# Key-value products beside the rows of the second layer, copied by ScalarE

## The chip, the cores and the metric

The kernel runs on one core of a Trainium2 chip. The metric is the device time of one execution in microseconds (us).

## The reference

Eight batches of eight heads, 576 positions, head size 64, go through an attention without softmax and a root-mean-square norm. The 8 x 576 = 4608 rows of 512 values that come out of it go through two dense layers with a gate.

```python
kv  = einsum('bhsd,bhse->bhde', k, v)            # 64x64 a head
out = einsum('bhsd,bhde->bhse', q, kv)
x   = out / sqrt(mean(out * out, -1) + 1e-6) * g_norm   # heads side by side: 4608 x 512
h   = x @ w_in                                   # 512 x 2048
y   = (h * sigmoid(1.702 * h)) @ w_out           # 2048 x 512
```

## The kernel before

**Stages.** Stage t = 0 to 8 (`for t in range(NT)`) computes both layers of 512 rows. Stages 0 to 7 take the first 512 positions of batch t; stage 8 takes the 64 remaining positions (the remainder) of all eight batches. Beside its layers, stage t does the attention of batch b = t + 1, so that its rows are ready when the next stage begins. Most of a stage is one long order of TensorE (PE) instructions, written out by hand: `at1(n, f)` puts work behind step n of the first layer, `at2(n, f)` behind step n of the second. Every engine takes its instructions in program order, and a wait on one holds back all that stands behind it on the same engine.

**First layer** (`hid_seven`, from stage 1 on). Seven products in place of eight, as in Strassen's scheme, for each of four groups of columns: 28 products of four matmuls of 256 columns. The list of a `Plan` names them: "21" is product 1 of group 2. Product 1 leaves a snapshot of its PSUM bank (copied by VectorE or ScalarE, letter by letter in `snap`) to which product 2 adds; product 5 leaves one for the sum that 6 completes; products 2, 3, 4 and 7 are followed by a gate on ScalarE (L539). `xsums` tells behind which steps VectorE forms the four sums of x (xS, L491); product 5 reads the first and product 6 the second. The word "kv" in the list is the place of the key-value products. `SECOND` is the plan of stage 1, `LATER` of stages 2 to 6, `LAST_TWO` of stages 7 and 8.

**Second layer** (`Seven.run`). Seven products of two halves of eight matmuls, 112 steps. `place` adds up and writes the output block; the last, behind step 111, is a ScalarE copy (L659). `ready` and `later` place VectorE's sums of the gated values (gS, L611).

**Attention of a batch from 2 on.** GpSimd's queue loads k, v and q as f16 (`load_kv`, `load_q`), into one buffer for k and one for v, and two for q, taken in turn. `transpose_q` turns q by a DMA of SP's queue. The 40 key-value products (L238: per head pair four blocks of 128 positions and the remainder, 128x64 weights, two heads side by side in the 64-column halves) go to one PSUM bank `kvp`. `keep_kv` copies it in four pieces into `kvd[b % 2]`. `rows` multiplies the turned q with it: 32 matmuls with 64x128 weights (L313) into four banks. ScalarE squares them (L323), VectorE adds up (`add_up`), ScalarE takes the reciprocal roots (`roots`, L338), VectorE scales (`turn`, L341), and two DMA transposes on SP's queue (L347) give `xT`, which the next stage reads. The remainder has its own path: `out` (L287), a square, `ss` (a matmul with ones, L358), a root on ScalarE (L360), `apply` on VectorE (L374), at steps 46, 74 and 80. Roots and gates need different tables of ScalarE, so that two `preload_act_table_set` stand in each second layer, the one for the gates at step 82.

**PSUM.** `ps_a` ("a") and `ps_h` ("h") have three banks each and `ps_o` ("o") two. `kvp`, one bank of the rows, the bank y of the second layer, `out`, `ss` and four banks of the first layer share `ps_a`.

**Where the moved work stands before.** For batch b, "kv" is the third entry of `LATER` (behind 21 and 01) and the 23rd of `SECOND`; the four copies follow on VectorE. Right behind, from step 15 (23) of the same first layer, stand `load_kv(t + 2)` and `load_q(t + 2)`; GpSimd holds them back until the products have read the buffers. The attention object of batch t + 2 is made and its q is turned at step 100 of the second layer.

Of the kernel before, what the change touches and what calls it, by code (L numbers as in the profile page):

```python
# [7 lines left out]
F16 = mybir.dt.float16  # L8
F32 = mybir.dt.float32
# [3 lines left out]
P = 128  # L13
# [3 lines left out]
def kernel(  # L17
# [52 lines left out]
    ident = const.tile([P, P], F16)  # L70
    ones2 = const.tile([P, P], F16)
    eps_t = const.tile([P, 1], F32)
    g_col = const.tile([P, 1], F32)
    w_in_sb = const.tile([P, KO, DFF], F16)
    w_out_sb = const.tile([P, FO, DM], F16)
# [32 lines left out]
    RW = J * D  # L108
    RS = H * RW

    def load_kv(b, h0=0, h1=H, rest=True):

        for n in "kv":
            nc.gpsimd.dma_start(  # L114
                out=kv_rows[n][:, h0 * RW : h1 * RW].rearrange("p (h x) -> p h x", x=RW),
                in_=srcs[n][b, h0:h1, 0:SM, :].rearrange("h (p j) d -> p h (j d)", j=J),
            )
        for n in "kv" if rest else "":
            nc.gpsimd.dma_start(
                out=kv_rows[n][0:R, RS : RS + H * D].rearrange("p (h d) -> p h d", d=D),  # L120
                in_=srcs[n][b, :, SM:S, :].rearrange("h p d -> p h d"),
            )

    def clear_rest():
        for n in "kv":
# [85 lines left out]
    class Attention:  # L211
# [3 lines left out]
        def __init__(self, b):  # L215
            self.b, self.kb = b, kvb[b] if b < EARLY else kvd[b % 2]
            self.qT, self.o = {}, {}
            x = xpool.tile([P, KO * SM], F16, name="xT", tag="xT")
            if b < EARLY:
                self.x = xT[b] = x.rearrange("p (c n) -> p c n", c=KO)  # L220
            else:
                self.x = x.rearrange("p (m r) -> p m r", r=P)
                xT[b] = x.rearrange("p (j c r) -> p c j r", j=J, c=KO)
                self.x16 = attn.tile([P, J, DM], F16, name="x16", tag="x16", bufs=1)

        def kv(self, c):
            if c % self.KEEP == 0:
# [18 lines left out]
        def early_kv_product(self, t, c):  # L246
            for j in range(NJ):
                for hl in range(2):
# [6 lines left out]
                        stop=(j == NJ - 1),  # L255
                    )

        def kv_all(self, engine):
            self.engine = engine
            for c in range(NPAIR):  # L260
                self.kv(c)

        def keep_kv(self, c0, c1):

# [24 lines left out]
        def out(self, c):  # L289
            pool, tag = (ps_a, "att") if c < NPAIR else self.rest_pool  # L290
            t = pool.tile([P, SM], F32, name="outT", tag=tag)
            if c < NPAIR:
                n = SM
                self.product(t, c)
            else:
                n = NPAIR * R
                for i in range(NPAIR):
                    self.rest_product(t[:, i * R : (i + 1) * R], i)
            t = t[:, 0:n]
            sq = attn.tile([P, SM], F16, name="sq", tag="sq", bufs=3)  # L300
            nc.scalar.activation(sq[:, 0:n], t, AFT.Square)
            self.o[c] = (t, sq, n)

        def rows(self, i):

            t = [
                pool.tile([P, DM], F32, name="outR", tag=tag)
                for pool, tag in ROW_BANKS[i]
            ]
            for h in range(H):  # L310
                for half in range(2):
                    r = slice(half * D, (half + 1) * D)
                    nc.tensor.matmul(  # L313
                        t[half][:, h * D : (h + 1) * D],
                        self.qTd[r, h * (J // 2) + i, :],
                        self.kb[r, h // 2, half, 1 - h % 2, :],
                        start=(h == 0),
                        stop=True,
                        skip_group_check=True,
                    )  # L320
            for half in range(2):
                sq = attn.tile([P, SM], F16, name="sq", tag="sq", bufs=3)
                nc.scalar.activation(sq, t[half], AFT.Square)  # L323
                self.o[2 * i + half] = (t[half], sq)

# [12 lines left out]
            nc.scalar.activation(s4, s4, AFT.Abs_reciprocal_sqrt, bias=eps_t, scale=1.0 / D)  # L338

        def turn(self, j):  # L340
            nc.vector.tensor_mul(  # L341
                self.x16[:, j, :].rearrange("p (h d) -> p h d", d=D),
                self.o[j][0].rearrange("p (h d) -> p h d", d=D),
                self.sum4[:, j, :].unsqueeze(2).to_broadcast([P, H, D]),
            )
            if j % 2:
                nc.sync.dma_start_transpose(  # L347
                    out=self.x[:, (j - 1) * KO : (j + 1) * KO, :],
                    in_=self.x16[:, j - 1 : j + 1, :].rearrange("p j n -> p (j n)"),
                )  # L350
# [541 lines left out]
    for fo in COLS[4:GROUP]:  # L892
# [28 lines left out]
        {'rows': (19, 19), 'add_up': (22, 26, 27, 31), 'table': 26, 'roots': (27, 33), 'turn': (40, 50, 51, 52)},  # L921
    )
    LATER = Plan(
# [4 lines left out]
        {1: 'DAAA', 5: 'AAAD'},  # L928
        "D",
        "aooa",  # L930
        "aahh",
        {15: '34'},
        (0, 1, 6, 11),
        {'rows': (15, 15), 'add_up': (17, 20, 24, 28), 'table': 24, 'roots': (28, 39), 'turn': (35, 38, 46, 48)},
    )
    LAST_TWO = Plan(
# [21 lines left out]
    for t in range(NT):  # L958
# [12 lines left out]
        if t == 0:  # L971
            for l in range(2):
                at1(6, nc.vector.memset, kvd[l], 0.0)
            at1(7, of(0, "out", NPAIR))
            at1(7, scale_w_in, 0, 4)
            at1(7, w_in_sums, 0, 2)
            at1(8, start, 1)
            at1(12, scale_w_in, 4, 6)
            at1(12, w_in_sums, 2, 3)
            at1(13, load_q, 2)  # L980
            at2(4, setattr, a0, "ss_pool", Attention.ss_pool)
            at2(4, of(0, "ss", NPAIR, True))
            at2(4, of(0, "apply", NPAIR))
            at2(18, weight_sum, 0, 0, HF)
            at2(18, scale_w_in, 6, 8)
            at2(18, w_in_sums, 3, 4)
            for c in range(NPAIR):
                at1(12, of(1, "pack_q", c))
                at2(9 + 3 * c, of(1, "q", c))
                at2((36, 36, 49, 49)[c], of(1, "kv", c))  # L990
                at2((41, 43, 54, 55)[c], of(1, "out", c))
                at2((45, 50, 58, 60)[c], of(1, "ss", c))
                at2((48, 52, 58, 62)[c], of(1, "apply", c))
            for n in range(1, 4):
                at2(19, weight_sum, n, 0, 4)
                at2(38, weight_sum, n, 4, 6)
            at2(39, load_kv, 2, 0, H // 2, False)
            at2(51, clear_rest)
            at2(51, load_kv, 2, H // 2, H)

            def first_sum():
                made[1] = Sums(1, xT[1])
                made[1].form(0)

            at2(55, first_sum)
        elif b < B:
            todo = plan(t)
            at1(todo.steps.index("kv"), of(b, "kv_all", todo.keep))
            if t == 1:
                at1(5, start, b)  # L1010
                at1(5, of(b, "transpose_q"))
                at1(4, nc.scalar.preload_act_table_set, "gelu_apprx_sigmoid_and_others")
                for n, i in ((1, 8), (2, 11), (3, 16)):
                    at1(i, weight_sum, n, 6, HF)
            if t + 2 < B:
                late = max(15, todo.steps.index("kv") + 1)
                at1(late, load_kv, t + 2)
                at1(late, load_q, t + 2)
                at2(100, start, t + 2)
                at2(100, of(t + 2, "transpose_q"))  # L1020
            at = todo.attn
            at2(at["table"], nc.scalar.preload_act_table_set, "abs_reciprocal_sqrt_and_small")
            for h in range(2):
                at2(at["roots"][h], of(b, "roots", h))
            for j in range(J):
                if j < J // 2:
                    at2(at["rows"][j], of(b, "rows", j))
                for name in ("add_up", "turn"):
                    at2(at[name][j], of(b, name, j))
            at2(46, of(b, "out", NPAIR))  # L1030
            at2(74, of(b, "ss", NPAIR))
            at2(80, of(b, "apply", NPAIR))
            at2(82, nc.scalar.preload_act_table_set, "gelu_apprx_sigmoid_and_others")
        elif t < B:
            for name in ("ss_pool", "rest_pool"):
                at2(16, setattr, live[1], name, (ps_a, "att"))
            at2(16, of(1, "out", NPAIR))
            at2(34, nc.scalar.preload_act_table_set, "abs_reciprocal_sqrt_and_small")
            at2(44, of(1, "ss", NPAIR))
            at2(50, of(1, "apply", NPAIR))  # L1040
            at2(52, nc.scalar.preload_act_table_set, "gelu_apprx_sigmoid_and_others")
# [31 lines left out]
```

## Time and profile before

| what | us |
|---|---|
| median of 3 runs | 259.71 |
| lowest, highest | 259.07, 260.14 |
| the profiled execution | 259.19 |
| its span in the trace | 257.4 |

The profile shows one execution. PE is the matmul, PEld the weight load that overlaps it, DVE is VectorE, ACT ScalarE, POOL GpSimd, SP SyncE; a "q" behind the name is the engine's queue of DMA issues. The granted clock of TensorE was 1.00 throughout. In the chain of waits a line is: start, length, engine and place, number of instructions. In a timeline it is the same with the operation, its operands and, in square brackets, the engine's idle time before it and who ended it; matmuls overlap, so that a timeline's group ends with its last matmul and the next group may start before. The chain counts a matmul from when its predecessor hands over, some 0.16 us after its start in the timeline. The lines on DMA issues end with the median time from issue to landing.

### The profile page before, as it was taken

To read this page: it belongs to the slowest core of one execution; us is meant where nothing else is said; L and a number is where in the kernel's file an instruction comes from. 1 tells how busy PE (TensorE), PEld (TensorE's weight loads), DVE (VectorE), ACT (ScalarE), POOL (GpSimd) and SP (SyncE) were. 2 spreads that over 40 slices of the span, in tenths; PEclk is the share of its full clock that TensorE was granted. 3 is DMA by queue.
4 is the path that set the end of the run, shared out by engine and by line. 5 is a ranking of instruction groups with operands and counts; after the bars stand their busy time and mean duration, and the time that the engine had idled before them with its cause. 6 is when DMAs were issued, how large, how long until landed. Compare 5 with 4: busy or idle time off the path is not lost.

```text
span 257.4 us, 6356 instructions
## 1 busy us (share of the span) xinstructions
PE 250.0 (97%) x2596; PEld 203.3 (79%) x2596; DVE 195.1 (76%) x351; ACT 175.0 (68%) x315; POOL 55.9 (22%) x85
## 2 busy tenths in 40 slices
PE   7889999999999999999999999999999999999994
PEld 2434454788888888888888888888888888888883
DVE  1565686899968896889689968996899687557842
ACT  3477834988749974997499748984799469836820
POOL 8963245107025002600160007000000000000013
PEclk9999999999999999999999999999999999999999
DMA  7999999999989947994799579957600430012005
GB/s 169 198 201 205 205 203 197 231 201 136 165 183 172 216 65 172 144 229 62 176 141 226 60 177 140 230 58 175 165 4 0 84 163 3 0 60 107 3 17 147
DMA packets 68671, 35.33 MB, mean 137 GB/s; under 512 B 37954, under 2 KB 66242, under 8 KB 68386
## 3 DMA queue, kind: packets, MB, share of 16 engines
q0 software_dynamic: 37616, 18.31, 54.9%
q1 hardware_dynamic: 30624, 16.29, 27.1%
q8 instruction: 20, 0.33, 0.5%
q10 hardware_dynamic: 402, 0.33, 0.4%
q14 instruction: 9, 0.07, 0.1%
HBM read 36.70 MB, written 9.44 MB: 179 GB/s over the span
## 4 chain that ended last, share of the span: by engine, by line
PE 92%; DMA 5%; POOL 1%; issue 0%; DVE 0%
PE o L679 38%; PE h L559 38%; PE o L794 5%; PE hT L452 5%; DMA w_in_sb<-in_moe_w_in_dram 3%; DMA qraw<-in_q_dram 2%; PE kvp L238 2%; PE outR L313 1%; PE ss L358 1%; POOL w_in_sb L171 0%; PE q L433 0%; PE kvp L250 0%; PE outT L283 0%; PE outT L287 0%; POOL vbuf L90 0%
## 5 line engine op out<-in xcount | busy, mean ns | idle before, releaser
L539 ACT ACTIVATE gT<-h 128x512 f16<-128x512 f32 x96 | 52.5, 602 | 5.4 <-PE h L559 5.3
L559 PEld LDWEIGHTS <-ws 128*128 128x128 f16 x512 | 50.1, 98 | 5.8
L679 PEld LDWEIGHTS <-gS 128*128 128x128 f16 x512 | 49.4, 98 | 6.2 <-DVE gS L611 0.3
L559 PE MATMUL h<-xS,ws 128*128 128x256 f16 x384 | 52.2, 273 | 0.0
L679 PE MATMUL o<-tw,gS 128*128 128x256 f16 x384 | 46.5, 273 | 0.0
L679 PEld LDWEIGHTS <-gT 128*128 128x128 f16 x384 | 37.6, 98 | 4.3
L559 PEld LDWEIGHTS <-w_in_sb 128*128 128x128 f16 x384 | 37.1, 98 | 4.7
L559 PE MATMUL h<-xT,w_in_sb 128*128 128x256 f16 x224 | 31.9, 273 | 0.0
L679 PE MATMUL o<-w_out_sb,gT 128*128 128x256 f16 x256 | 31.4, 273 | 0.0
L573 DVE TENSOR_TENSOR h<-h,s 128x512 f32<-128x512 f32 x32 | 22.2, 697 | 6.7 <-PE h L559 5.5
L114 POOL DMA_DIRECT2D kraw<-in_k_dram x7 | 6.0, 855 | 90.4 <-PE kvp L238 86.2
L575 DVE TENSOR_TENSOR s<-h,s 128x512 f32<-128x512 f32 x32 | 22.1, 691 | 4.1 <-PE h L559 3.3
L656 DVE TENSOR_TENSOR osb<-o,qf 128x512 f32<-128x512 f32 (+1 forms) x25 | 16.7, 668 | 11.2 <-PE o L679 8.3
L713 POOL DMA_DIRECT2D out_dram<-osb x6 | 3.2, 541 | 90.9 <-DVE osb L656 90.9
L611 DVE TENSOR_TENSOR gS<-gT 128x512 f16<-128x512 f16 (+2 forms) x32 | 21.2, 684 | 0.6 <-ACT gT L539 0.6
L539 ACT ACTIVATE gT<-s 128x512 f16<-128x512 f32 x32 | 19.8, 628 | 2.6 <-DVE s L575 2.5
L559 PE MATMUL h<-xS,w_in_sb 128*128 128x256 f16 x128 | 18.9, 273 | 0.0
L360 ACT ACTIVATE rs<-ss,eps_t 128x512 f32<-128x512 f32 (+1 forms) x16 | 9.2, 582 | 13.6 <-PE ss L358 13.5
L966 ACT ACT_TABLE_LOAD x14 | 18.0, 1283 | 0.3
L648 ACT COPY qf<-o 128x512 f32<-128x512 f32 (+1 forms) x26 | 14.2, 547 | 4.5 <-PE o L679 4.4
L329 DVE TENSOR_REDUCE sum<-sq 128x8 f32<-128x512 f16 x24 | 15.3, 679 | 2.5 <-ACT sq L323 2.5
L509 ACT COPY h<-h 128x512 f32<-128x512 f32 x27 | 15.6, 585 | 2.1 <-PE h L559 2.0
(100 smaller groups left out, 361.0 us busy)
## 6 DMA issues: line engine op xcount, KB each, us to landing
out_dram<-osb SPq DMA_DIRECT2D x8, 512.0 KB, 3.8
kraw<-in_k_dram POOLq DMA_DIRECT2D x5, 512.0 KB, 9.2
vbuf<-in_v_dram POOLq DMA_DIRECT2D x5, 512.0 KB, 12.2
out_dram<-osb SPq DMA_DIRECT2D x2, 1024.0 KB, 4.9
qraw<-in_q_dram POOLq DMA_DIRECT2D x3, 512.0 KB, 13.5
qbuf<-in_q_dram POOLq DMA_DIRECT2D x3, 512.0 KB, 13.5
out_dram<-osb SPq DMA_DIRECT2D x6, 192.0 KB, 5.6
w_in_sb<-in_moe_w_in_dram POOLq DMA_DIRECT2D x2, 512.0 KB, 10.8
```

Of the source, the lines that this page charges most:

```text
L329: nc.vector.tensor_reduce(out=self.sum4[:, j, :], in_=self.o[j][1].rearrange("p (x d) -> p x d", d=D), op=ALU.add, axis=mybir.AxisListType.X,)
L452: nc.tensor.matmul(self.h[fo], w_in_sb[:, ko, fo * P : (fo + 1) * P], self.x[:, ko], start=(ko == 0), stop=(ko == KO - 1),)
L509: (nc.vector.tensor_copy if engine == "D" else nc.scalar.copy)(to, src)
L539: nc.scalar.activation(self.gT[:, to, n * TH : (n + 1) * TH], src, AFT.Gelu_apprx_sigmoid)
L559: nc.tensor.matmul(bank[name][:, a], w, x, start=(p in (1, 5) and a == 0 and k == 0), stop=(k == KH - 1), skip_group_check=True,)
L573: nc.vector.tensor_add(bank["z"], bank["x"], self.s5)
L575: nc.vector.tensor_add(self.s5, bank["x"], self.s5)
L611: op(s[:, n, lo], a, b)
L648: nc.scalar.copy(self.kept[as_][:, m], ps)
L656: nc.vector.tensor_add(o, ps, self.kept[with_][:, m])
L679: nc.tensor.matmul(o, a, w, start=(p in (1, 2, 5) and i == 0 and (mo == 0 or split)), stop=(i == HF - 1), skip_group_check=True,)
L966: u2.setdefault(i, []).append(lambda: f(*args))
```

## The change

The products of batches 4 to 7 move from the first layer of stages 3 to 6 to step 15 of the second layer of stages 2 to 5, directly ahead of the rows of batches 3 to 6. Their bank is copied at step 52, by ScalarE. Batch 3 has its products and copies (by ScalarE) at step 88 of stage 1's second layer; batch 2 stays where it is. In `LATER`, "kv" is gone and 25 stands ahead of 22; the second roots come at step 29 (before: 39), and one of VectorE's gS sums at 29 (before: 22). In stages 2 to 5 the remainder's four steps move from 46, 74, 80, 82 to 80, 90, 96, 97. The loads change their place: k of batch t + 3 behind the products at step 15, then at step 101 a one-element GpSimd copy that reads the last block of the turned rows (`after_turn`, so that the queue waits for that transpose), and behind it v, the two remainders and q. The squares get a fourth buffer, and `x16` is allocated with its first use.

```diff
-    def load_kv(b, h0=0, h1=H, rest=True):
+    def load_kv(b, h0=0, h1=H, rest=True, main="kv"):
-        for n in "kv":
+        for n in main:
...
+    def after_turn(b):
+        nc.gpsimd.tensor_copy(out=mark, in_=xT[b].rearrange("p c j r -> p j c r")[0:1, J - 1, KO - 1, 0:1])
...
+        def kv_products(self):
+            self.kvp = ps_a.tile([P, NPAIR, D], F32, name="kvp", tag="att")
+            for c in range(NPAIR):
+                self.kv_product(self.kvp[:, c, :], c)
+        def kv_copies(self, engine):
+            self.engine = engine
+            self.keep_kv(0, NPAIR)
         def kv_all(self, engine):
-            self.engine = engine
-            for c in range(NPAIR):
-                self.kv(c)
+            self.kv_products()
+            self.kv_copies(engine)
...
     LATER = Plan(
-        "21 01 kv 22 05 25 06 11 02 15 26 03 16 12"
+        "21 01 25 22 05 06 11 02 15 26 03 16 12"
         " 07 31 27 13 17 35 36 04 23 24 32 33 14 37",
-        {23: ((0, 4, 0), (0, 4, 1)), 26: ((4, 6, 0),)},
-        {0: ((0, 8, 2),), 16: ((4, 8, 1),), 22: ((4, 8, 3),), 58: ((0, 4, 3),)},
+        {22: ((0, 4, 0), (0, 4, 1)), 25: ((4, 6, 0),)},
+        {0: ((0, 8, 2),), 16: ((4, 8, 1),), 29: ((4, 8, 3),), 58: ((0, 4, 3),)},
...
-        (0, 1, 6, 11),
+        (0, 1, 5, 10),
-        {..., 'roots': (28, 39), ...},
+        {..., 'roots': (28, 29), ...},
...
-            at1(todo.steps.index("kv"), of(b, "kv_all", todo.keep))
+            at = todo.attn
             if t == 1:
+                at1(todo.steps.index("kv"), of(b, "kv_all", "D"))
...
+                at1(22, load_kv, 3)
+                at1(22, load_q, 3)
+                at2(88, start, 3)
+                at2(88, of(3, "kv_all", "A"))
+                at2(89, load_kv, 4)
+                at2(89, load_q, 4)
+            elif t + 2 < B:
+                at2(at["rows"][0], start, t + 2)
+                at2(at["rows"][0], of(t + 2, "kv_products"))
+                at2(52, of(t + 2, "kv_copies", "A"))
+                if t + 3 < B:
+                    at2(at["rows"][0], load_kv, t + 3, 0, H, False, "k")
+                    at2(101, after_turn, b)
+                    at2(101, load_kv, t + 3, 0, H, True, "v")
+                    at2(101, load_q, t + 3)
             if t + 2 < B:
-                late = max(15, todo.steps.index("kv") + 1)
-                at1(late, load_kv, t + 2)
-                at1(late, load_q, t + 2)
-                at2(100, start, t + 2)
                 at2(100, of(t + 2, "transpose_q"))
...
+            rest = (80, 90, 96, 97) if 1 < t < B - 2 else (46, 74, 80, 82)
+            at2(rest[0], of(b, "out", NPAIR))
+            at2(rest[1], of(b, "ss", NPAIR))
+            at2(rest[2], of(b, "apply", NPAIR))
+            at2(rest[3], nc.scalar.preload_act_table_set, "gelu_apprx_sigmoid_and_others")
```

More of the change, by code (lines that the diff above doesn't have):

```diff
@@ L72 @@
     eps_t = const.tile([P, 1], F32)
+    mark = const.tile([1, 1], F16)
     g_col = const.tile([P, 1], F32)
@@ L223, in __init__ @@
                 xT[b] = x.rearrange("p (j c r) -> p c j r", j=J, c=KO)
-                self.x16 = attn.tile([P, J, DM], F16, name="x16", tag="x16", bufs=1)
         def kv(self, c):
@@ L299, in out @@
             t = t[:, 0:n]
-            sq = attn.tile([P, SM], F16, name="sq", tag="sq", bufs=3)
+            sq = attn.tile([P, SM], F16, name="sq", tag="sq", bufs=4)
             nc.scalar.activation(sq[:, 0:n], t, AFT.Square)
@@ L321, in rows @@
             for half in range(2):
-                sq = attn.tile([P, SM], F16, name="sq", tag="sq", bufs=3)
+                sq = attn.tile([P, SM], F16, name="sq", tag="sq", bufs=4)
                 nc.scalar.activation(sq, t[half], AFT.Square)
@@ L340, in turn @@
         def turn(self, j):
+            if j == 0:
+                self.x16 = attn.tile([P, J, DM], F16, name="x16", tag="x16", bufs=1)
             nc.vector.tensor_mul(
@@ L932 @@
         {15: '34'},
-        (0, 1, 6, 11),
-        {'rows': (15, 15), 'add_up': (17, 20, 24, 28), 'table': 24, 'roots': (28, 39), 'turn': (35, 38, 46, 48)},
+        (0, 1, 5, 10),
+        {'rows': (15, 15), 'add_up': (17, 20, 24, 28), 'table': 24, 'roots': (28, 29), 'turn': (35, 38, 46, 48)},
     )
@@ L1014 @@
                     at1(i, weight_sum, n, 6, HF)
+                at1(22, load_kv, 3)
[13 more added lines that the diff above has]
+                    at2(101, load_q, t + 3)
             if t + 2 < B:
-                late = max(15, todo.steps.index("kv") + 1)
-                at1(late, load_kv, t + 2)
-                at1(late, load_q, t + 2)
-                at2(100, start, t + 2)
                 at2(100, of(t + 2, "transpose_q"))
-            at = todo.attn
             at2(at["table"], nc.scalar.preload_act_table_set, "abs_reciprocal_sqrt_and_small")
@@ L1029 @@
                     at2(at[name][j], of(b, name, j))
[L1030 to L1033, printed above, removed]
+            rest = (80, 90, 96, 97) if 1 < t < B - 2 else (46, 74, 80, 82)
[3 more added lines that the diff above has]
+            at2(rest[3], nc.scalar.preload_act_table_set, "gelu_apprx_sigmoid_and_others")
         elif t < B:
```

## The prediction

> **What bounds the kernel.** I read the page first: the engines' shares, then the chain that ended last.
>
> ```profile
> span 257.4 us, 6356 instructions
> PE 250.0 (97%) x2596; PEld 203.3 (79%) x2596; DVE 195.1 (76%) x351; ACT 175.0 (68%) x315; POOL 55.9 (22%) x85
> PE 92%; DMA 5%; POOL 1%; issue 0%; DVE 0%
> PE o L679 38%; PE h L559 38%; PE o L794 5%; PE hT L452 5%; DMA w_in_sb<-in_moe_w_in_dram 3%; DMA qraw<-in_q_dram 2%; PE kvp L238 2%; PE outR L313 1%; PE ss L358 1%; POOL w_in_sb L171 0%; PE q L433 0%; PE kvp L250 0%; PE outT L283 0%; PE outT L287 0%; POOL vbuf L90 0%
> ```
>
> PE carries 92% of the chain; what the DMAs hold (5%) lies at the head, which the change doesn't touch. Next I read the chain in order of time, for one whole stage (t = 5):
>
> ```profile
> 152.18 0.87 PE h L559 x8
> 153.05 0.75 PE kvp L238 x40
> 153.81 11.02 PE h L559 x100
> ...
> 167.01 0.57 PE outR L313 x32
> ...
> 174.36 4.04 PE o L679 x37
> 178.40 0.87 PE h L559 x8
> ```
>
> One stage is 178.40 - 152.18 = 26.22 us, and PE stands in every piece of it, those left out too. A matmul of a layer takes 11.02 / 100 = 0.110 us or 4.04 / 37 = 0.109 us, so nothing waits between them. The change issues the same matmuls. It can gain only where PE loses time without waiting for another engine, and it can lose wherever it makes PE wait. So I read PE's timeline around the products and around the rows, and how long one of their matmuls lasts:
>
> ```profile
> 125.80 1.04 PE L559 MATMUL h<-xT,w_in_sb 128*128 128x256 f16 x8
> 126.77 0.82 PE L238 MATMUL kvp<-vbuf,kraw 128*64 128x64 f16 x40
> 127.52 0.61 PE L559 MATMUL h<-xT,w_in_sb 128*128 128x256 f16 x4
> ...
> 140.19 0.60 PE L559 MATMUL h<-xS,w_in_sb 128*128 128x256 f16 x4
> 140.73 0.64 PE L313 MATMUL outR<-kvd,qTd 64*128 64x64 f16 x32
> 141.30 0.83 PE L679 MATMUL o<-tw,gS 128*128 128x256 f16 x6
> ```
> ```profile
> L238 PE MATMUL kvp<-vbuf,kraw x240: 196/196/217, 56.2 to 179.8; 128*64 128x64 f16 x120
> L313 PE MATMUL outR<-kvd,qTd x192: 190/190/200, 62.4 to 193.6; 64*128 64x64 f16 x192
> ```
>
> The forms differ: the layers load 128*128 weights, the products 128*64, the rows 64*128. Eight layer matmuls from 125.80 fill 8 x 0.109 = 0.87, to 126.67; the products start at 126.77, 0.10 later. Their row ends 0.82 after its start and one lasts 0.196, so the last of the 20 pairs starts at 127.39: 19 steps in 0.62, 0.033 each. The next layer matmul comes 0.13 after that pair, 0.10 more than a step. Into the rows: 140.19 + 4 x 0.109 = 140.63 against 140.73, 0.10 again. Out of them: the last starts at 140.73 + 0.64 - 0.19 = 141.18, a step is 0.45 / 15 = 0.03, the next at 141.30: 0.09 over. So each change of form costs PE 0.10 us, and a stage has four.
>
> **The change, part by part.** *Products beside the rows (batches 4 to 7).* 40 matmuls leave the first layer and stand directly ahead of the 32 rows. In and out of the products and of the rows were four changes; three are left if products to rows counts as one. The trace has no 128*64 beside 64*128. Its bounds are no cost (two changes saved, 0.20 us a batch) and two changes (nothing saved). The nearest row is a direct step between two small forms at the head:
>
> ```profile
> 7.46 0.38 PE L250 MATMUL kv<-vbuf,kraw 96*64 96x64 f16 x12 [0.27 <-DVE vbuf L835]
> 7.77 0.28 PE L858 MATMUL g_ps<-one_t,g_row 1*64 1x1 f32 x4
> ```
>
> The last of the twelve starts at 7.46 + 0.38 - 0.196 = 7.64, the next form at 7.77: 0.13, the same 0.10 over a step of 0.03. So I take one change, 0.10 saved, four times: **-0.4 us**, with bounds 0 and -0.8. The Trainium skill (TensorEngine Tiling (Array Packing), Key Properties) says that changing the tiling mode, not just the tile, drains TensorE; by it the step from products to rows keeps its drain, and the trace agrees as far as the row at 7.77 goes. TensorE: Matmul & The Clock Gate of the Trainium skill (step-by-step, drain) gives about 128 cycles for one, an estimate of 0.05 us; the sum by it would be -0.2. The rows show 0.10.
>
> *Batch 3* moves from stage 2's first layer to step 88 of stage 1, between layer matmuls as before: 0. Its loads are issued from 57.29 in both versions, since GpSimd waits for batch 2's products:
>
> ```profile
> 57.29 0.89 POOL L114 DMA_DIRECT2D kraw<-in_k_dram  x1 [10.54 <-PE kvp L238]
> 59.81 0.69 POOL L119 DMA_DIRECT2D vbuf<-in_v_dram  x1
> 71.61 2.06 SPq L273 DMA_TRANSPOSE qTd<-qbuf  x1
> 73.53 0.88 PE h L559 x8
> ```
>
> Step 88 comes 23 x 0.109 = 2.5 before 73.53, at 71.0. The q load, issued last, has let its transpose start at 71.61, and at the page's median (11.4, below) the last key-value piece would land at 71.2. A stall of 0 to 0.2, once; I take 0.
>
> *The first layer, 0.85 us shorter, and its copies.* The four copies of 0.42 us each leave VectorE there (1.7 us a batch) and land on ScalarE at step 52, so neither engine has more to do per matmul in the first layer. What the products covered is the start of it:
>
> ```profile
> 152.22 0.59 ACT L659 COPY osb<-o 128x512 f32<-128x512 f32 x1 [2.26 <-PE o L679]
> 152.70 0.59 ACT L509 COPY h<-h 128x512 f32<-128x512 f32 x1
> 153.70 0.41 DVE L491 TENSOR_TENSOR xS<-xT,xS 128x512 f16<-128x512 f16 x1
> ```
>
> These belong to the layer that starts on PE at 125.80 + 26.22 = 152.02. Product 22 needs the snapshot that ends at 153.29. It stood after 21, 01 and the products; now it is the fourth product (25 is put ahead of it), due at 152.02 + 3 x 0.437 = 153.33. Product 06 needs the xS that ends at 154.11 and is due at 152.02 + 5 x 0.437 = 154.20. Margins of 0.04 and 0.09: less the hand-over, a stall of 0 to 0.06 in each of five layers. I take 0.1 in all. Without 25 ahead, 22 would wait 0.4 each time.
>
> *ScalarE's copies at step 52 and the remainder moved from 46-82 to 80-97.* ScalarE has this idle time late in the stage:
>
> ```profile
> 148.18 0.47 ACT L360 ACTIVATE rs<-ss,eps_t 128x256 f32<-128x256 f32 x1 [1.69 <-PE ss L358]
> 148.67 1.28 ACT L966 ACT_TABLE_LOAD   x1
> L648 ACT COPY qf<-o 128x256 f32<-128x256 f32 x4 | 1.5, 371 | 0.8 <-PE o L679 0.8
> L509 DVE CAST kvd<-kvp 64x256 f16<-64x256 f32 x24 | 10.1, 421 | 0.2
> ```
>
> A ScalarE copy of 256 columns is 0.37; four are 1.5 us, in the 1.69 that it waited before 148.18: hidden. The `ss` product moves by 16 steps, 1.75 us: the root starts at 149.9, the table load ends at 149.9 + 0.47 + 1.28 = 151.7, ahead of the osb copy at 152.22 by 0.5. Hidden; without that margin it goes into 22 one for one. The second roots, now at step 29, only wait for the last sum sooner than they did.
>
> *Loads.* k of batch t+3 is issued after the products at step 15, v, the remainders and q after the turned rows have landed.
>
> ```profile
> kraw<-in_k_dram POOLq DMA_DIRECT2D x5, 512.0 KB, 9.2
> vbuf<-in_v_dram POOLq DMA_DIRECT2D x5, 512.0 KB, 12.2
> qraw<-in_q_dram POOLq DMA_DIRECT2D x3, 512.0 KB, 13.5
> vbuf<-in_v_dram POOLq DMA_DIRECT2D x6, 64.0 KB, 11.4
> 146.41 2.75 SPq L347 DMA_TRANSPOSE xT<-x  x2
> DMA to landing us min/median/max: 3.1/3.2/4.9
> ```
>
> The second transpose starts halfway through its row, at 147.8, and lands at 151.0, 1.0 before 152.02. GpSimd then issues v and k's remainder (0.89 + 0.69, as at 57.29 and 59.81, and the mark), and at 152.7 the last piece, which at its median lands at 164.1. It is needed at the next step 15: 152.02 + 27 x 0.437 + 15 x 0.109 + 0.44 = 165.9. Margin 1.8: hidden. The queue was free of loads earlier, so k meets little at step 15.
>
> Sum: -0.4 + 0.1 = -0.3. The profiled execution took 259.19 (span 257.4 and 1.8 around it), which would become 258.9. The median of the runs is 259.71, 0.5 above it, so I forecast **259.4**. A measurement of this kernel can tell about 0.5% (1.3 us) from no change; this is well inside.
>
> **The rivals.** *Two changes saved*: products and rows run through with no drain, -0.8, median 258.9. For it: both are small forms whose weights load in pairs. Against: the 0.10 at 7.77. *Nothing saved*: the mixed step costs two, 259.8.
>
> *Slower: the remainder's tail reaches the next layer.* Place: root, table load, osb copy, snapshot of 21, product 22, all in ScalarE's order. Margin 0.5 at the osb copy, then 0.04. Each further delay of the root counts in the four boundaries after stages 2 to 5. It passes the 1.3 us when the root starts after 149.9 + 0.5 + (1.3 + 0.3) / 4 = 150.8; late by a whole table load, it costs 4 x (1.28 - 0.5) = 3.1, 262.5. For it: `out`, its square, `ss` and root follow each other within 10 steps, 1.1 us. Against: a square of 256 columns is of the size of that 0.37 copy, and ScalarE is otherwise empty there.
>
> *Slower: v late at step 15*, for batches 5 to 7. It decides from 13.2 us to landing (11.4 + 1.8). At q's 13.5 it costs 3 x 0.3 = 0.9, 260.3; at 14.5, 3 x 1.3 = 3.9, 263.3. For it: v now meets the q transpose and both stores. Against: it no longer stands behind k in the queue, which was issued first and landed in 9.2.
>
> **How the numbers follow.** Forecast 0.63, nothing saved 0.05, two saved 0.08, tail 0.11 (0.07 of it past 1.3 us), late v 0.09 (0.07 past it), and 0.04 for a gain past 1.3 us: it would need 0.33 a batch, more than the 0.20 of two changes, and I can't place the rest. So faster 0.04, slower 0.14, same 0.82. The range goes from two changes saved less the runs' own spread (258.6) to either slower case at about half a us a boundary, 261.2.
>
> **What would show it.** Right: the rows start 0.13 after the last pair of products with no layer matmul between, a stage of 26.1, PE without a wait from 47 on. Wrong: idle PE at product 22 with the snapshot as releaser (tail), at L238 with a v load as releaser (loads), or products to rows with no gap or 0.2. A stage longer than 26.3 disproves the forecast.

## The result, and the profile after

The changed kernel takes 260.88 us (median of 6 runs, 260.53 to 261.38), the kernel before 259.29 beside it (6 runs, 259.07 to 260.14): ratio 1.0057, 95% interval 1.0039 to 1.0075. The forecast was 259.4, a gain of 0.3 against the runs shown with it; the change costs 1.6. The time lies inside the range given (258.6 to 261.2), on the side that had a chance of 0.14, but that is luck: the upper end was set by two rivals (a late tail on ScalarE, a late v) and neither of them came. The profiled execution took 260.70, its span is 258.9.

The page after, its first lines and the shares of the chain by engine and line:

```profile
span 258.9 us, 6351 instructions
PE 250.2 (97%) x2596; PEld 203.8 (79%) x2596; DVE 186.6 (72%) x331; ACT 183.6 (71%) x335; POOL 56.2 (22%) x88
...
PE 86%; DMA 11%; DVE 1%; issue 0%; ACT 0%; POOL 0%
PE o L693 37%; PE h L573 33%; DMA qTd<-qraw 6%; PE o L808 5%; PE hT L466 5%; DMA qraw<-in_q_dram 2%; DMA vbuf<-in_v_dram 2%; PE kvp L242 1%; PE outR L325 1%; PE ss L372 1%; PE outT L295 0%; PE kvp L254 0%; PE q L447 0%; DVE xT L382 0%; PE o
```

20 fewer VectorE instructions, 20 more on ScalarE, as the diff says. New is the DMA share, 11% for 5%, and within it one transfer that was not there: the transpose of q, 6% of the span. The chain in order of time shows where (start, length, what):

```profile
98.17 1.78 PE o L693 x17
99.95 16.35 DMA qTd<-qraw
116.30 0.05 issue
116.34 0.64 PE outR L325 x32
...
127.80 11.85 PE h L573 x108
...
141.83 0.75 PE kvp L242 x40
142.58 0.57 PE outR L325 x32
...
153.96 6.12 PE h L573 x56
```

The rows of stage 3 begin when the turned q of batch 4 lands, at 116.30. One stage later the rows don't wait: products and rows follow each other, and the stage is 153.96 - 127.80 = 26.16 us. Behind the head, the view of PE's waits lists one (in total, times, longest):

```profile
PE outR L325 <- DMA qTd<-qraw: 1.1, 1, 1.1
```

The lengths of the stages, each from the first matmul of its first layer to the next stage's, and the tail from the last matmul's start to the span's end, worked out from the two traces:

```
stage       1      2      3      4      5      6      7      8     tail
before  26.47  26.22  26.22  26.22  26.22  26.22  24.68  24.35   3.95
after   27.33  26.12  27.34  26.17  26.12  25.37  24.68  24.34   4.62
change  +0.86  -0.10  +1.12  -0.05  -0.10  -0.85   0     -0.01  +0.67
```

Stage 1 gains the products of batch 3, stage 6 has none left, and these two cancel. Stages 2 and 5 show the gain that was forecast, 0.10 each. Stage 3 would too, but for 1.2 us of waiting. The tail is 0.67 longer. The sum is 1.5, the difference of the two spans.

PE's timeline shows the step from products to rows in stage 2:

```profile
88.25 0.82 PE L242 MATMUL kvp<-vbuf,kraw 128*64 128x64 f16 x40
89.00 0.64 PE L325 MATMUL outR<-kvd,qTd 64*128 64x64 f16 x32
```

The last pair of products starts at 88.25 + 0.82 - 0.196 = 88.87, the rows 0.13 later: one change of form.

**Why q's transpose is late.** The queues of SP and GpSimd around the end of stage 2, first before, then after (start, length of the issue, what):

```profile
99.24 3.72 SPq L273 DMA_TRANSPOSE qTd<-qraw  x1
101.64 0.90 POOL L114 DMA_DIRECT2D kraw<-in_k_dram  x1 [20.95 <-PE kvp L238]
```
```profile
98.99 0.18 POOL L127 COPY mark<-xT 1x1 f16<-1x1 f16 x1 [8.75 <-DMA xT<-x]
99.23 0.88 POOL L115 DMA_DIRECT2D vbuf<-in_v_dram  x1
99.95 3.52 SPq L285 DMA_TRANSPOSE qTd<-qraw  x1
101.44 0.91 POOL L139 DMA_DIRECT2D qbuf<-in_q_dram  x1
```

Before, the transpose went out 2.4 us ahead of the first load. After, the v load goes out 0.7 ahead of the transpose, because both are now released at almost the same time: the loads by the landing of the turned rows, the transpose by step 100. What the DMA engines moved in 3 us while the transposes were under way, by queue (packets, MB, share of 16 engines), q1 being SP's queue and q0 GpSimd's: before from 101 to 104, after from 110 to 113, and after from 103.3 to 106.3:

```profile
q1 hardware_dynamic: 2068, 0.59, 111.8%
q0 software_dynamic: 8, 0.00, 2.0%
```
```profile
q0 software_dynamic: 632, 0.32, 86.3%
q1 hardware_dynamic: 635, 0.16, 57.7%
```
```profile
q0 software_dynamic: 1023, 0.44, 125.9%
q1 hardware_dynamic: 33, 0.01, 1.5%
```

Without loads beside it, SP's queue moves 2068 packets in 3 us; from 110 to 113, with loads, it moves 635, one for each packet of the loads. The Trainium skill (DMA: Bandwidth & Descriptors, Queues, rings and completion order) says that a DMA engine takes turns between its queues packet by packet; 632 against 635 agrees. A transpose in many small packets (0.16 MB / 635 = 250 bytes) loses by even turns against loads with packets twice that size (0.32 MB / 632 = 510 bytes). Even turns are not all of it, though: from 103.3 to 106.3 the loads moved 1023 packets and SP's queue 33. The transpose's own packets (256 bytes each) begin 6.1 us after its issue here, and 1.9 us after it in the kernel before. So about 4 us were lost before its first packet, and why SP's queue stood still so long isn't shown.

From issue to landing, minimum, median and maximum of the transposes of stages 2 to 5, before and after (the landing of stage 1's isn't recorded; stage 5's, the 5.0, has no loads beside it):

```profile
DMA to landing us min/median/max: 6.6/8.1/9.0
```
```profile
DMA to landing us min/median/max: 5.0/11.7/16.4
```

The rows of stage 3 would start at about 115.1 (14.8 us into a stage that began at 100.29, as in stage 2), so that the transpose has some 15.2 us. Before, it used 9.0 of them at most. Now it takes 10 to 16 beside the loads, and whether PE waits is decided by the last microsecond.

**Why the tail is longer.** The DMA queues in the last 3 us or so (from 0.9 us behind the last matmul's start to the end), and the landing of the last two stores, before and after:

```profile
q10 hardware_dynamic: 197, 0.15, 18.0%
q1 hardware_dynamic: 162, 0.13, 15.3%
q0 software_dynamic: 32, 0.07, 7.0%
...
out_dram<-osb SPq DMA_DIRECT2D x1, 64.0 KB, 2.0
out_dram<-osb ACTq DMA_DIRECT2D x1, 64.0 KB, 2.2
```
```profile
q14 instruction: 1, 0.01, 1.1%
...
out_dram<-osb SPq DMA_DIRECT2D x1, 64.0 KB, 2.7
out_dram<-osb ACTq DMA_DIRECT2D x1, 64.0 KB, 2.9
```

The stores land 0.7 later, and a packet of instructions (queue q14, 8 KB, 0.6 us) stands among them, 1.95 us after the start of the last matmul. There are nine such packets in either kernel; before, the last one came at 236.2, 17 us ahead of that matmul. In both traces this last packet comes when VectorE has begun the 447th instruction that the trace records of it (semaphore instructions counted); VectorE's list had 475 of them and has 450 now. So the packet moved from 28 instructions ahead of the end to 3. Over all fourteen traces it comes with VectorE's 444th to 449th recorded instruction, so it goes with VectorE's list.

### The profile page after: what moved, and what is told of

It reads as the page before. It is cut to its first block, busy times and chain, and to the rows that moved or that the text cites. A ratio compares the mean times of both kernels' runs of the same rounds, so it can differ in the third digit from the quotient of the medians.

```text
span 258.9 us, 6351 instructions
## 1 busy us (share of the span) xinstructions
PE 250.2 (97%) x2596; PEld 203.8 (79%) x2596; DVE 186.6 (72%) x331; ACT 183.6 (71%) x335; POOL 56.2 (22%) x88
## 4 chain that ended last, share of the span: by engine, by line
PE 86%; DMA 11%; DVE 1%; issue 0%; ACT 0%; POOL 0%
PE o L693 37%; PE h L573 33%; DMA qTd<-qraw 6%; PE o L808 5%; PE hT L466 5%; DMA qraw<-in_q_dram 2%; DMA vbuf<-in_v_dram 2%; PE kvp L242 1%; PE outR L325 1%; PE ss L372 1%; PE outT L295 0%; PE kvp L254 0%; PE q L447 0%; DVE xT L382 0%; PE outT L299 0%
## 5 line engine op out<-in xcount | busy, mean ns | idle before, releaser
L573 PE MATMUL h<-xS,ws 128*128 128x256 f16 x384 | 53.0, 273 | 0.0
L693 PE MATMUL o<-tw,gS 128*128 128x256 f16 x384 | 45.6, 273 | 0.0
L313 ACT ACTIVATE sq<-outT 128x512 f16<-128x512 f32 (+1 forms) x16 | 7.8, 490 | 14.8 <-PE outT L295 9.3
```

Source lines behind the costliest of these rows:

```text
L573: nc.tensor.matmul(bank[name][:, a], w, x, start=(p in (1, 5) and a == 0 and k == 0), stop=(k == KH - 1), skip_group_check=True,)
L693: nc.tensor.matmul(o, a, w, start=(p in (1, 2, 5) and i == 0 and (mo == 0 or split)), stop=(i == HF - 1), skip_group_check=True,)
```

## The experiments

The first theory: stage 3's wait is the price of loads that go out together with the transpose; without it the kernel is faster than before. Rivals: the transpose is late by its own place in SP's queue, whatever the loads do; the gain of 0.10 comes from elsewhere, not from the form of the weights; the tail belongs to the copies or the squares that were moved.

**e1: the loads behind the turned q.** The loads of step 101 wait for the landing of q's transpose instead of the turned rows'.

```diff
+    def after_q(b):
+        nc.gpsimd.tensor_copy(out=mark, in_=live[b].qTd[0:1, 0, 0:1])
-                    at2(101, after_turn, b)
+                    at2(101, after_q, t + 2)
```

> The changed kernel with one edit: GpSimd's one-element copy at step 101 reads the turned q of batch t + 2 and not the turned rows of batch t + 1, so that v, the remainders and q are loaded only when that transpose has landed. Theory 1 (the q transpose is late because its packets take turns with those loads): it lands within 9 us of its issue in every stage, the wait at the rows of stage 3 is gone, and the time is 0.3 to 0.5 us under the kernel before (about 258.9), if v still comes in time. Theory 2 (the q transpose is late because SP's queue has the first half of the output ahead of it): nothing changes on SP, the transpose still takes 13 to 16 us, about 260.9. Theory 3 (the loss is at the end of the stages, on ScalarE and in the last stores, and the wait in stage 3 is an accident of one execution): still about 260.9 with no wait in stage 3. If v is late instead: PE waits at the products of stages 3 to 5, above 260.

260.19 us (12 runs), ratio 1.0032, 1.0016 to 1.0048. The chain of e1 over the same stretch:

```profile
100.61 11.80 PE h L577 x108
...
114.59 0.75 PE kvp L246 x40
115.34 0.57 PE outR L329 x32
...
126.73 8.31 PE h L577 x76
```
```profile
DMA to landing us min/median/max: 5.0/5.2/6.7
```

The transposes land in 5 to 7 us, no row waits, and stages 2 to 5 are all 126.73 - 100.61 = 26.12. The wait is settled: it was the loads. But the time is 0.7 below the changed kernel's and still above the kernel before, where 258.9 was expected: the tail is 4.86, and the packet stands 2.15 behind the start of the last matmul.

**e2: q's load early.** Only the q load leaves step 101; v and the remainders stay there.

```diff
-                    at2(101, load_q, t + 3)
+                    at2(0, load_q, t + 3)
```

> The changed kernel with q of batch t + 3 loaded at step 0 of the second layer of stages 2 to 4 instead of behind v; v and the remainders stay behind the turned rows. Theory 1: the q transpose still takes turns with v and the remainders, but these are 0.65 MB and not 1.2 MB, and so it lands 10 to 12 us after its issue; it is needed 14.3 us after, no wait, about 258.9 to 259.2. Theory 2: 13 to 16 us as in the changed kernel, about 260.9. Theory 3: about 260.9.

260.27 us, ratio 1.0036 (1.0008 to 1.0064). The transposes still take up to 13.4 us, beside v and the remainders alone, but that is in time for the rows. The time misses what was expected (258.9 to 259.2): the tail is 4.82, and one wait of 0.4 for xS stands in stage 4.

**e3: the transpose earlier.** q is turned at step 79 instead of 100 in stages 2 to 5, ahead of the loads.

```diff
-                at2(100, of(t + 2, "transpose_q"))
+                at2(79 if t > 1 else 100, of(t + 2, "transpose_q"))
```

> The changed kernel with the q transpose at step 79 instead of 100 in stages 2 to 5: on SP's queue it then stands ahead of the store of the first half of the output and is issued some 2.5 us sooner, ahead of the loads behind the turned rows. Theories 1 and 2: it lands within 8 us, no wait at the rows, about 258.9; a later store costs nothing. Theory 1 alone has the transposes of the rows unchanged at 3.1 to 3.3 us. Theory 3: about 260.9.

260.51 us, ratio 1.0053 (1.0033 to 1.0073). Landing 4.9 to 6.0 us; stages 2 to 5 are 26.12. In the profiled execution (261.29) the products of batch 3 waited for v's load, in a stage that the edit leaves alone, so that no verdict on the time can be drawn from it:

```profile
PE kvp L242 <- DMA vbuf<-in_v_dram: 1.3, 1, 1.3
```

All three ways of parting transpose and loads take the wait away; so the transpose isn't late by its own place in SP's queue.

**e4: products apart from the rows.** The products stand at step 12, three layer matmuls and four more ahead of the rows.

```diff
-                at2(at["rows"][0], start, t + 2)
-                at2(at["rows"][0], of(t + 2, "kv_products"))
+                at2(12, start, t + 2)
+                at2(12, of(t + 2, "kv_products"))
```

> The changed kernel with the products (and the making of the attention object) at step 12 of the second layer instead of 15, so that layer matmuls stand between products and rows. If a change of form costs 0.10 us and the products beside the rows saved one a batch: a stage without a wait takes 26.22 us as in the kernel before and not 26.12, and the time is 0.4 us above the changed kernel, about 261.3. If the saving in the changed kernel came from elsewhere: 26.12 and 260.9. The wait at the rows of stage 3 stays under theories 1 and 2, since the loads and transposes keep their places; under theory 3 it need not show again.

PE's timeline of e4 in stage 3:

```profile
114.77 1.47 PE L693 MATMUL o<-w_out_sb,gT 128*128 128x256 f16 x12
116.17 0.82 PE L242 MATMUL kvp<-vbuf,kraw 128*64 128x64 f16 x40
116.92 0.50 PE L693 MATMUL o<-w_out_sb,gT 128*128 128x256 f16 x3
117.26 0.60 PE L573 MATMUL h<-xS,w_in_sb 128*128 128x256 f16 x4
117.79 0.64 PE L325 MATMUL outR<-kvd,qTd 64*128 64x64 f16 x32
```

Twelve layer matmuls fill 12 x 0.109 = 1.31 to 116.08, the products start 0.09 later; their last pair starts at 116.79, the next matmul 0.13 later. Four changes again, and the stages 3, 4 and 5 are 26.23 each, 0.11 above the 26.12 of the products beside the rows. So the 0.10 goes with the change of form. The time, 262.52 (ratio 1.0096, 1.0064 to 1.0128), isn't explained by that: 0.7 us are two waits for v in stage 2, since the products come earlier there, and stage 1 begins 1.5 us later than in the changed kernel, ahead of everything that the edit touches. In the profiled execution (262.54) the granted clock of TensorE was 0.64 from 14 to 18 us, where the changed kernel had 1.00. Four of the six runs took 262.5 to 262.8 with a mean clock of 0.987 to 0.991, the other two 260.4 and 260.9 with 0.998, so the median says nothing about 0.4 us.

**e5 and e6: a longer VectorE list.** 24 one-element VectorE memsets stand in the head, in e5 on top of e1, in e6 on top of the change alone. They do no work of the kernel.

```diff
+    pad_t = const.tile([1, 1], F32)
+    for _ in range(24):
+        nc.vector.memset(pad_t, 0.0)
```

> The first experiment (loads behind the turned q) with 24 VectorE memsets of one element added at the head, where VectorE waits for the first loads. In it and in the changed kernel the time from the last matmul to the end is 4.6 to 4.9 us, against 3.95 in the kernel before, and one 8 KB packet of the instruction queue (q14) starts some 2 us after the last matmul, where the last stores are under way; before it starts 17 us ahead of it. Both times it comes when VectorE has started its 447th record, and the change took 25 of VectorE's records away. Theory A (this fetch of VectorE's instructions stands on one of the stores' DMA engines): the 24 memsets move it back to about 235 us, the tail is 3.9 to 4.1, and the time 0.9 less than the first experiment: 259.3, with PE's stages as there (26.12), at or up to 0.4 under the kernel before. Theory B (the tail is longer because of other addresses, ScalarE's or GpSimd's longer lists, or the order of the loads): the tail stays at 4.6 to 4.9, and the time at 260.2.

> The changed kernel with the same 24 memsets and nothing else. Theory A: the tail goes from 4.6 to about 4.0, the wait at the rows of stage 3 stays as it falls out (0 to 1.6 us): about 260.0, 0.9 under the changed kernel. Theory B: 260.9. If both this and the loads' place count as thought, the four kernels add up: changed 260.9, loads behind q 260.2, memsets 260.0, both 259.3.

e5: 259.01 us against 259.30, ratio 0.9995 (0.9973 to 1.0017). e6: 259.53, ratio 1.0005 (0.9992 to 1.0018). Each memset version is 1.2 to 1.35 below the same kernel without them. The last packet comes at 236.2 and 236.1, the tail is 3.96 in both. The end of e1 and of e5 in the view of the DMA queues (from 0.99 and 0.96 us behind the start of the last matmul):

```profile
q14 instruction: 1, 0.01, 0.9%
...
out_dram<-osb SPq DMA_DIRECT2D x1, 64.0 KB, 2.9
out_dram<-osb ACTq DMA_DIRECT2D x1, 64.0 KB, 3.1
```
```profile
out_dram<-osb SPq DMA_DIRECT2D x1, 64.0 KB, 1.9
out_dram<-osb ACTq DMA_DIRECT2D x1, 64.0 KB, 2.2
```

The single packets show how the fetch holds up the stores. In e1 the packet of instructions starts at 255.36 and takes 0.57 us, to 255.93. By 255.81 all packets of the last stores have started but ten, five of each queue. The same view from 255.87 (2.66 behind the start of the last matmul) to the end lists these ten; in e5 nothing is left from 256.08 (2.64 behind) on:

```profile
q1 hardware_dynamic: 5, 0.00, 1.1%
q10 hardware_dynamic: 5, 0.00, 1.0%
```
```profile
DMA packets 0, 0.00 MB, mean 0 GB/s; under 512 B 0, under 2 KB 0, under 8 KB 0
```

The first of the ten starts at 255.93, where the packet of instructions ends, and the others follow it one by one. In the changed kernel, e2, e3 and e4 there are ten late packets too. The first starts 2.56, 2.64, 2.62 and 2.63 us behind the start of the last matmul, and the packet of instructions ends at 2.57, 2.64, 2.62 and 2.64. Five times out of five, a part of both stores waits for the end of this packet.

e6 has the change's loads and the change's slow transpose, up to 15.3 us, but its rows wait 0.2 where the changed kernel's waited 1.1: the wait varies from one execution to the next. How the difference of the medians divides between the tail and the wait isn't shown.

**e7, e9 and e12: a shorter VectorE list in the kernel before.** In the kernel before, the copies of the products are left out from batch 3, 2 and 1 on (20, 24 and 28 instructions).

```diff
         def keep_kv(self, c0, c1):
+            if self.b > 2:
+                return
```

> The kernel before with the copies of the key-value products of batches 3 to 7 left out (20 VectorE instructions less, so that the rows of these batches are computed from zeros). Nothing else moves; VectorE's list becomes as long as in the changed kernel. Theory A: the instruction packet that started 17 us before the last matmul starts near the last stores, the tail grows from 3.95 to 4.6 to 4.9, and the time rises by 0.7 to 0.9 to about 260.0 although there is less work; PE's stages stay at 26.22. Theory B: the tail stays at 3.95 and the time at 259.2.

> The kernel before with the copies of the key-value products of all batches from 2 on left out (24 VectorE instructions less; the rows of these batches are computed from zeros). With batch 2's four kept, VectorE had 455 records, and the instruction packet started at 251.4, two us ahead of the last matmul and clear of the last stores; here it should have 451, and the packet comes four VectorE instructions later, at 253.5 to 255.5. Theory A (a fetch beside the last stores delays their landing): the tail grows from 3.96 to 4.5 to 4.9 and the time by 0.6 to 0.9, to about 260.0, with PE's stages still 26.22. Theory B (the fetch only goes along with something else in the changed kernels): the tail stays at 3.96 and the time at 259.3.

> The kernel before, without the 28 copies of the key-value products of batches 1 to 7 (those outputs are computed from zeros), so that VectorE's list is 28 instructions shorter and the work of TensorE the same. Theory (place of the last packet of instructions): the packet moves from 236 to about 255, beside the last stores, and the kernel before gets the changed kernel's tail, 4.6 to 4.9 where it had 3.96; median 260.0, ratio 1.003. Rival (the tail's length belongs to something else in the change): tail 3.96, median 259.1.

259.37, 259.06 and 259.16 us, each the same as before (ratios 1.0010, 0.9995, 0.9992, intervals across 1). The packet did move, from 236.2 to 251.4, 251.6 and 258.0, but each time clear of the last stores: 2.0 and 1.5 us ahead of the last matmul's start, and 4.6 behind it, when the stores have landed and the span is over. The tails are 3.96, 3.96 and 3.94. All three miss what was expected of them: it came with the 448th, 444th and 448th record of VectorE, and up to some us behind it, so that the count places it only roughly. They bear out that a packet clear of the stores costs nothing, and don't show the reverse, a kernel before with a long tail.

**e11: six memsets.** As e5, with 6 for 24.

> The changed kernel with the loads behind the turned q, and six one-element memsets at VectorE's head in place of 24. Theory (the last packet of instructions comes with about the 447th recorded instruction of VectorE, and costs the tail only when that stands beside the last stores): with six more instructions the 447th stands where the 441st stood, at 250; the packet at about 251.5, 4 us ahead of the last stores; tail 3.96, median 259.0 to 259.3, ratio 0.999. Rival (the length of the tail has another cause, and the 24 memsets helped in the head): the tail stays at 4.8 and the median at 260.2. The stages 2 to 5 are 26.12 either way.

259.42 us (11 runs), ratio 1.0013 (1.0004 to 1.0022). The packet came at 251.1, where it was expected, and 0.8 us of e1's loss is gone with six instructions that do nothing. The tail of the profiled execution was 4.45 though, where 3.96 was expected: the last stores landed 0.2 to 0.3 later than in e5, and GpSimd's closing drain ended 0.5 later. The packet, 1.9 us ahead of the last matmul, can't have held these stores; a VectorE addition began 0.35 later there than in e5, counted from the last matmul, and with it GpSimd's last stores went out 0.35 later. Why that addition was late isn't shown; a tail can be long without the packet, too.

Over all traces the tail goes with the packet:

```
last packet, from the start of the last matmul     kernels                 tail
+1.95 to +2.33 us (beside the last stores)         after, e1 to e4         4.62 to 4.86
-17.3 to -17.2                                     before, e5, e6, e8, e10 3.95 to 3.96
-2.0, -1.5, +4.6                                   e7, e9, e12             3.96, 3.96, 3.94
-1.9                                               e11                     4.45
```

**e8 and e10: two variants of e5.** e8 has e4's products apart, e10 has e3's early transpose.

> The loads behind q and the 24 memsets, with the products at step 12 and the rows at step 15, so that they are two excursions again. If a change of form costs 0.10 us: stages 2 to 5 of 26.23 in place of 26.12, and 0.4 us more than the kernel with both edits and products beside the rows, about 259.7. If not: no difference. v is needed 0.3 us sooner here, and a wait for it at the products would show in the profile.

> The loads behind the turned q and the 24 memsets, and in stages 2 to 5 the q transpose at step 79, ahead of the store of the first half, so that it lands, and the loads start, some 2.5 us sooner. If what is left to gain is the changes of form (0.4) and nothing else waits: 258.8 to 259.0, every one of stages 2 to 5 at 26.12, tail 3.96. If v's landing was still marginal in the kernel without this edit, its median comes down by 0.1 to 0.3; if not, it stays at 259.0.

e8: 260.78 us, ratio 1.0078 (1.0060 to 1.0097). Its stage 2 is 26.23, the 0.11 of e4 once more; the others hold waits for v (0.4) and xS (0.6), so that the 1.8 us over e5 are mostly not the form of the weights. e10: 259.43 us, ratio 1.0005 (0.9991 to 1.0018); the transposes land in 4.4 to 5.8 us, which e5 had no more use for. Stage 2 is 26.49 and not 26.12, with a wait of 0.2 for v, and a wait of 0.3 for xS stands at the start of stage 6, so the 258.8 to 259.0 expected was missed.

The best version, e5, is 0.3 below the kernel before in its median, and the interval doesn't tell it from no change.

## Why the prediction was wrong

The prediction's own sign of being wrong, a stage longer than 26.3, came: stage 3 is 27.34. But PE idled at neither of the places that it named for a loss, product 22 and the products' wait for v; it idled at the rows. The 0.5 that the forecast added for the median above the profiled execution was too much as well: over the six runs beside it is 0.1.

*Change of form, four times -0.10:* right in mechanism and size. Stages 2 and 5 lost 0.10, all four of e1 did, and e4 gave it back. The one step from products to rows costs 0.10, neither nothing nor two changes, so both of those rivals fell.

*Batch 3 at step 88, 0:* right. +0.86 in stage 1, -0.85 in stage 6, and no wait at its products in the changed kernel.

*Snapshots, +0.1:* the margins of 0.04 and 0.09 held. The 108 layer matmuls took 11.80 us in e1, 0.1093 each, with nothing to wait for; the term was 0. In the changed kernel PE lost 0.05 in stage 4 (11.85), at a product whose own need the sum didn't look at: 25, now the third, needs the first xS, which is formed when the turned rows have landed. In e2, e3, e8 and e10 PE waits 0.3 to 0.6 at that product, in one stage each.

*ScalarE's tail:* the forecast's table load was to end 0.5 ahead of the osb copy. It did, at 126.03 + 1.28 = 127.31 against 127.83 in ScalarE's timeline, and the copy waited for PE:

```profile
126.03 1.28 ACT L980 ACT_TABLE_LOAD   x1
127.83 0.58 ACT L673 COPY osb<-o 128x512 f32<-128x512 f32 x1 [0.52 <-PE o L693]
```

That rival, the one with the largest chance on the slower side, didn't come.

*Loads, "hidden":* this is the step that failed. It priced the landing of the loads that were moved, and v was indeed in time: v landed in 8.9 us at the median and no product waited for it in stages 2 to 5 (from the view of DMA issues, with the median to landing last):

```profile
vbuf<-in_v_dram POOLq DMA_DIRECT2D x5, 512.0 KB, 8.9
```

The rival of a late v even said that v "now meets the q transpose", and then asked only what that does to v. What it does to the transpose wasn't asked. The nearest row stood in the trace, 9.0 us at most against a need of 15, a margin of 6, but it was taken with the transpose 2.4 us ahead of the first load. Behind v's load it took up to 7 us more, and PE waited 1.1 us at the rows. e1, e2 and e3 show that it is this.

*What was not in the sum at all:* the end of the kernel. The prediction moved 20 instructions off VectorE and took that as free, as VectorE isn't the bound. It also moved the place at which its instructions are fetched. The trace of before had the nine packets on its page, and the stores at the end as a part of the span that no engine hides. Five kernels have the packet beside the last stores and a tail of 4.6 to 4.9; e5 and e6, which differ from e1 and the changed kernel by the memsets alone, have neither. That the packet delays the stores is shown by the ten late packets in each of the five traces. That it is the only thing that the memsets change isn't shown: they give 1.2 and 1.35 us, the profiled tails 0.9 and 0.7, and in e6 the wait of stage 3 was smaller as well. What decides the packet's place to the instruction stays open.

With both taken away, the four stages of e5 are shorter by 0.10 each, so the terms of the sum held in PE's own time. That e5's median lies 0.3 below the kernel before, as the sum had it, may be luck: the interval includes no change, its span in the trace is the same (257.4), since the head took 0.3 us more there, and e10 and e11 stand 0.08 and 0.15 above the kernel before.

## What to carry to other kernels

When a transfer is moved, price the transfers that it now meets, not only its own landing: put each queue's issues of the new order on one line of time, and ask of every transfer which bytes now go ahead of it and beside it. A landing read from the trace is a bound only for the order in which it was measured: the transposes took at most 9.0 us ahead of the loads and 16.4 behind v's, against a need of 15.2. Where a change shortens or lengthens an engine's list, look at where its packets of instructions fall and whether the last stores stand there; an effect of 0.7 us there is larger than the gain of 0.4 that was sought.

## What the runs showed of the hardware

A transpose by DMA of 512 KB landed in 5.0 to 6.7 us when the loads waited for it (e1), and in 10 to 16.4 beside them in the changed kernel, where SP's queue moved 635 packets in 3 us in place of 2068, and 33 in an earlier 3 us.

The last 8 KB packet of instructions took 0.3 to 0.6 us. Where it stood beside the last two stores of 64 KB, ten of their packets started only when it had ended, and the stores landed 0.7 to 1.0 later than without it. The Trainium skill (Runtime: NRT & Kernel Launch, Instruction fetch mechanics) says that the fetch goes through a queue of its own and is mostly hidden; the traces agree for the packets inside the stages (in the kernel before, stages 3, 5 and 6 hold one or two, stages 2 and 4 none, and all are 26.22 us), and for the last packet, where it stands beside the last stores, they don't.

One change of the weights' form costs PE 0.10 us, and two small forms next to each other, 128x64 and 64x128, pay it too.
